# A retention layer feeding a mixer MLP on one core: U ahead of two loads, w1 held and begun narrow, batch 0 in another order

## The chip, the core and the metric

The kernel runs on one core of a Trainium2 chip. A core has five engines with queues of their own, each working through its instructions in the order in which they were written: PE (TensorE, matrix products into PSUM), DVE (VectorE), ACT (ScalarE), POOL (GpSimd) and SP (SyncE, which here only issues DMAs). Semaphores order the engines among each other. The metric is the device time of one execution in microseconds (us); lower is better. The kernel before took 230.05 us (median of 3 runs, 228.76 to 230.13).

## What is computed

Eight heads of 64 columns attend with a decaying state; what comes out is x, 4 batches of 768 positions by 512 columns, and goes through a low-rank mixing over positions and a two-layer MLP with residual:

```python
for t in range(S):                                     # S = 768, H = 8, D = 64
    state = gamma * state + outer(k[:, :, t], v[:, :, t])
    y[:, :, t] = (q[:, :, t] @ state) / sqrt(D)
x  = heads of y side by side                           # 4 x 768 x 512
u  = x + ((x^T @ U) @ V)^T                             # U 768 x 32, V 32 x 768
out = u + relu(u @ w_ch1) @ w_ch2                      # 512 x 2048, 2048 x 512
```

All inputs and the output are float32 in DRAM; the kernel computes in bfloat16 with float32 sums.

## The kernel before

The recurrence is done in chunks: within a chunk by scores between q and k with a mask, across chunks by a state that is carried in PSUM. The decay is put in by scaling k or v by `gk` and q (or x) by `gq`.

Batch 0 is handled apart, since nothing can hide it. It is cut into six units: unit u is a group of four heads (units 0 to 2 and 3 to 5) by 256 positions. `load_unit` puts the loads of k, q and v of each unit, 256 KB each, on SP's queue, in the order of a written string, and U follows as the last. The string `STEPS` then gives all the work of batch 0 in the order in which it is put on the engines, and `BY` says for each step which engine takes it (A is ACT, D is DVE, P is POOL). The steps, with u the unit:

- `Ku`, `Qu`, `Vu` (`cast_unit`): cast the loaded tile to bfloat16; scaled by `gk2` or `gq2` on the way (a two-operand instruction, L83) or plain (L81, L77). The strings `scaled` and `ks` in `BY` say which: q of a unit is scaled where `scaled` has 1, and x is scaled instead where it has 0; k is scaled where `ks` has 1, else v. An S in the V row splits the cast between POOL and DVE (step `Wu`).
- `Tku`, `Tqu`: turn k and q by four matmuls each; `kTu`, `qTu`: bring them out of PSUM.
- `Su`: scores, 16 matmuls into the PSUM pair `R[u % 2]`; `mu`: masks them (DVE, L536).
- `STu.c`, `su.c`: add the half chunk c to the state; bring the state out.
- `Mu`: mix, i.e. state times q and masked scores times v (for unit 5 the part with the state is `N5`, after the rest); `xu`: brings x out.
- `xtc`, `P0`, `P1`, `R2`, `pc0`, `pc2`, `Ec`, `uc`: the low-rank mixing of batch 0, which makes the transposed u that the MLP reads; `Ub` casts U, `Va`, `Vb`, `Vc` bring V into bfloat16 in four copies.
- `Fs:n` (`fill`): n matmuls of zeros by zeros into a tile that step s will write, which keep PE working while it would wait.
- `w0`, `w1`: issue the loads of the columns of `w_ch1` on POOL (`load_w1`, L203). Ahead of the first one a one-element copy, the gate (L691), reads a loaded tile and so holds the load until that tile has landed.
- `B1`, `B2` (`begin_up`, L358): the first matmuls of the MLP of batch 0.

After the steps POOL issues the rest of `w_ch1`, then `w_ch2` in four parts (L208), and then a one-element copy from column 1023 of `w1b` into an input buffer (L712). SP's loads of batch 1 come after it: `feed_more(gate)` writes into that buffer. So batch 1's input starts when POOL has come past its issues and column 1023 has landed. POOL then casts each chunk of 128 positions of batch 1 (`prep`: kd, qd, vd; L81 and L83).

The MLP of a batch is a list of pieces (`mlp_pieces`), each of four matmuls with a cost of 0.864 or 0.432: 16 for the first 512 positions (L380), 16 for the last 256, and 24 of the second layer (L403). `weave` goes through the pieces and puts in, at marks that are fractions of the total cost, the attention of the next batch: `turn_chunk` (L230 for batch 1), `score`, `mix`, and the steps of the mixing. `AT` has for each batch the place of the first score, the step between chunks, and the leads of mix, prep and turn. The store of an output chunk is issued on POOL (L366) one piece after the chunk is complete.

Of the kernel before, what the change touches and what calls it, by code (L numbers as in the profile page):

```python
# [16 lines left out]
def kernel(  # L17
# [11 lines left out]
    nc = tc.nc  # L29
    P = 128  # L30
    B, H, S, D = q.shape
# [26 lines left out]
    R = [psum.tile([P, 2, 512], fp32, tag=f"r{g}", name=f"r{g}") for g in range(2)]  # L58
# [9 lines left out]
    def evac(eng, dst, src):  # L68
        if eng == "A":
            nc.scalar.activation(dst, src, AF.Copy)  # L70
        else:
            nc.vector.tensor_copy(out=dst, in_=src)
# [12 lines left out]
    Ub = wts.tile([P, NCK, RK], bf16)  # L85
    V4 = wts.tile([P, S], bf16)
    w1b = wts.tile([P, NCB, DH], bf16)
# [6 lines left out]
    ready = {}  # L94
    n_in = [0]

    def ring():
        n_in[0] += 1
        return rin.tile([P, 512], fp32, tag="in", name=f"in_{n_in[0]}")

    V1 = wts.tile([RK, S], fp32)
    Uf = wts.tile([P, NCK, RK], fp32)
    nc.sync.dma_start(out=V1, in_=moe_V)

    def load_unit(nm, u):
        g, b0 = UNITS[u]
        t = ready[nm, u] = ring()
        nc.sync.dma_start(
            out=t.rearrange("p (h x) -> p h x", h=HG),
            in_=src_of[nm][0, ds(HG * g, HG), ds(256 * b0, 256), :].rearrange(  # L110
                "h (t j) d -> t h (j d)", j=2))

    for step in ("k0 q0 v0 k1 q1 v1 k2 q2 v2 k3 q3 v3 k4 q4 k5 q5 v4 v5 ").split():
        load_unit(step[0], int(step[1]))
    nc.sync.dma_start(out=Uf, in_=moe_U.rearrange("(j p) r -> p j r", p=P))

    feed = [(nm, b, ci) for b in range(1, B) for ci in range(NCK) for nm in "kqv"]
    n_fed, n_held, n_open = [0], [0], [6 * NCK]
# [14 lines left out]
    def ramp(shape, pattern, mult):  # L133
        n_ramp[0] += 1
        t = consts.tile(shape, fp32, name=f"ramp{n_ramp[0]}")
        nc.gpsimd.iota(t, pattern=pattern, base=0, channel_multiplier=mult,
                       allow_small_or_imprecise_dtypes=True)
        return t
# [20 lines left out]
    s2 = ramp([P, 1], [[0, 1]], 2)  # L159
# [39 lines left out]
        for nm in "kqv":  # L199
            prep(nm, b, ci)  # L200

    def load_w1(mb):
        nc.gpsimd.dma_start(  # L203
            out=w1b[:, :, ts(mb, 512)],
            in_=moe_w_ch1[:, ts(mb, 512)].rearrange("(c p) n -> p c n", p=P))

    def load_w2(j):
        nc.gpsimd.dma_start(  # L208
# [236 lines left out]
    def part(f, *args):  # L445
        return lambda: f(*args)
# [5 lines left out]


    BY = {
             "K": "APADPP",
             "Q": "DDPPPD",
             "scaled": "000010",
             "ks": "010010",
             "V": "PASPDP",
             "kT": "ADAAAA",  # L460
             "qT": "AAAAAA",
             "x": "DDDDAA",
             "s": "AADAAA",
             "pc": "ADA",
             "u": "AAAD",
    }
    STEPS = (
        "Va K0 Q0 Vb Tk0 Vc Tq0 FS0:4 kT0 V0 qT0 S0 K1 ST0.0 FTk1:2 m0 s0.0 "
        "ST0.1 Tk1 s0.1 Q1 M0 V1 kT1 Tq1 ST1.0 FS1:2 qT1 x0 K2 S1 Q2 m1 s1.0 "
        "Tk2 ST1.1 kT2 V2 Tq2 s1.1 W2 M1 qT2 K3 ST2.0 x1 Tk3 S2 FTq3:1 Q3 kT3 "  # L470
        "s2.0 Tq3 FS3:4 m2 V3 qT3 S3 ST3.0 m3 K4 M2 s3.0 ST3.1 s3.1 Q4 Tk4 x2 "
        "M3 FTq4:1 kT4 K5 x3 Tq4 FTk5:1 qT4 Tk5 FTq5:1 Q5 w0 Tq5 kT5 S4 V4 xt0 "
        "w1 qT5 m4 ST4.0 xt1 s4.0 V5 S5 Ub ST4.1 m5 M4 s4.1 ST5.0 x4 P0 M5 s5.0 "
        "pc0 N5 E0 x5 P1 u1 xt2 R2 xt3 u0 pc2 E2 E3 u2 B1 u3 B2 "
    )
    eb = {}
    LAST = NCK - 1
# [1 line left out]
    def cast_unit(nm, u, eng, h0=0, nh=HG):  # L479
        g, b0 = UNITS[u]  # L480
        if (nm, u) not in eb:
            eb[nm, u] = rpre.tile([P, 2, HG, D], bf16, tag=nm + "d",
                                  name=f"{nm}u_{u}")
        src = ready[nm, u].rearrange("p (h j d) -> p j h d", h=HG, j=2)
        scale = gk2 if nm == "kv"[BY["ks"][u] == "0"] else None
        if nm == "q" and BY["scaled"][u] == "1":
            scale = gq2
        hs = ds(h0, nh)
        if scale is not None:
            scale = scale[:, b0, ds(HG * g + h0, nh)].rearrange("p h j -> p j h")  # L490
            scale = scale[:, :, :, None].to_broadcast([P, 2, nh, D])
        cast(eng, eb[nm, u][:, :, hs], src[:, :, hs], scale)
# [24 lines left out]
    def fill(nm, u, n):  # L517
        t = R[u % 2][:, 0] if nm == "S" else turn_bank(nm[1], u)
        for _ in range(n):
            nc.tensor.matmul(t, zeros[:, :P], zeros, start=True, stop=True)  # L520
# [100 lines left out]
    def pc_out(g, eng):  # L621
        rows = ds(2 * RK * g, 2 * RK)
        evac(eng, pcs[0][rows], xT["p"][rows, :P])
# [7 lines left out]
    def step(s):  # L631
        if s[0] == "F":
            s, n = s[1:].split(":")
            return fill(s[:-1], int(s[-1]), int(n))
        if s == "Va":
            return nc.gpsimd.tensor_copy(out=V1b, in_=V1)
        if s == "Vb":
            for i, n in enumerate((512, 256)):
                nc.tensor.matmul(R[1][:, i, :n], rep4, V1b[:, ds(512 * i, n)],
                                 start=True, stop=True)  # L640
            return
        if s == "Vc":
            return evac("D", V4, R[1].rearrange("p i n -> p (i n)")[:, :S])
        nm, at = s.rstrip("0123456789."), s.lstrip("KQVWTkqSmsMNxtPpcERUbuwB")
        u = int(at[0]) if at else 0
        eng = BY[nm][u] if nm in BY and nm != "pc" else None
        if nm in ("K", "Q", "V"):
            if eng == "S":
                cast_unit("v", u, "P", 0, 2)
            else:  # L650
                cast_unit(nm.lower(), u, eng)
        elif nm == "W":
            cast_unit("v", u, "D", 2, 2)
        elif nm in ("Tk", "Tq"):
            turn_unit(nm[1], u)
        elif nm in ("kT", "qT"):
            turned_unit(nm[0], u, eng)
        elif nm == "S":
            score_unit(u)
        elif nm == "m":  # L660
            mask_unit(u)
        elif nm == "ST":
            state_unit(u, int(at[2]))
        elif nm == "s":
            state_out(u, int(at[2]), eng)
        elif nm == "M":
            mix_unit(u)
        elif nm == "N":
            query_unit(u, False)
        elif nm == "x":  # L670
            x_out(u, eng)
        elif nm == "Ub":
            evac("A", Ub, Uf)
        elif nm == "xt":
            x_turn(u)
        elif nm == "P":
            proj(u, range(NCK if u == 0 else 4))
        elif nm == "R":
            proj(1, range(4, NCK))
        elif nm == "pc":  # L680
            pc_out(u // 2, BY["pc"][u // 2])
        elif nm == "E":
            expand((0, 1) if u == 0 else (u,))
        elif nm == "B":
            for m in range(2):
                begin_up(m, (0, 1) if u == 1 else (2,))
        elif nm == "u":
            evac(eng, uTs[0][:, u, :LO], xT[u][:, :LO])
        elif nm == "w":
            if u == 0:  # L690
                nc.gpsimd.tensor_copy(out=gate0, in_=ready["q", 5][:1, :1])  # L691
            load_w1(u)
        else:
            raise ValueError(s)

# [7 lines left out]
    gate0 = consts.tile([1, 1], fp32)  # L703
    pieces0 = mlp_pieces(0)
    for s in STEPS.split():
        step(s)
    for mb in range(2, 4):
        load_w1(mb)
    for j in range(4):
        load_w2(j)  # L710
    gate = ring()
# [4 lines left out]
    for ci in range(3):  # L716
        prep_chunk(1, ci)

    AT = {1: (0.47, 0.068, 0.045, 0.07, 0.04), 2: (0.20, 0.085, 0.05, 0.20, 0.12),
          3: (0.13, 0.10, 0.05, 0.20, 0.12)}  # L720
    LR = (0.71, 0.75, 0.83, 0.89)
    marks = {b: [] for b in range(B)}
# [1 line left out]
    def mark(at, f, *args):  # L724
        marks[int(at)].append((at % 1.0, part(f, *args)))
# [5 lines left out]
    for b in range(1, B):  # L731
        s0, step, dm, dp, dt = AT[b]
        for ci in range(NCK):
            s_at = b - 1 + s0 + step * ci
            if (b, ci) >= (1, 3):
                mark(s_at - dp, prep_chunk, b, ci)
            mark(s_at - dt, turn_chunk, b, ci)
            mark(s_at, score, b, ci)
            mark(s_at + dm, mix, b, ci)
            if b > 2:  # L740
                mark(b - 2 + 0.25 + 0.1 * ci, open_chunk)
        if b == 1:
            mark(0.885, lr_open, b)
            mark(0.885, lr_proj_turn, b)
            mark(0.925, lr_uT, b)
            mark(1.11, lr_expand, b, 0, 4)
        else:
            l0, l1, l2, l3 = LR
            mark(b - 1 + l0, mixed, b)
            mark(b - 1 + l1, lr_expand, b, 0, 4)  # L750
            mark(b - 1 + l2, lr_turn, b, 0)
            mark(b - 1 + l3, lr_turn, b, 2)
        mark(b + 0.02, lr_expand, b, 4, 2)
        mark(b + 0.06, lr_turn, b, 4)
# [35 lines left out]
```

## Time and profile before

One execution was profiled:

| | |
|---|---|
| time of the profiled execution | 229.61 us |
| its span in the profile | 227.8 us |
| median of the 3 timed runs | 230.05 us |
| PE busy in the first 5, second 5, third 5 us | 3.81, 4.76, 4.03 us |
| PE busy, 25 to 30 and 30 to 35 us | 4.87, 5.00 us |
| loads of k, q, v, issue to landing | 4.5, 4.8, 4.6 us (median) |
| loads of w1, issue to landing | 8.2 us (median of 4) |
| loads of w2, issue to landing | 17.6 us (median of 4) |

In the views that follow, a line of the timeline has start and length in us, the engine, the line of the kernel, the operation, the tile written and the tile read with their shapes, how many instructions were merged, and in brackets the idle time of the engine ahead of it with what ended that. Names are those of the tiles: ku, qu, vu are casts of batch 0, kd, qd, vd those of later batches, a the masked scores. The page's rows in tenths cut the span into 40 slices of 5.7 us.

### The profile page before, as it was taken

How to read it: one execution, taken by the hardware profiler on the slowest of the kernel's cores; microseconds unless marked ns; L12 is line 12 of the kernel's file. 1: busy time of each engine (PE TensorE's matmuls, PEld its weight loads, DVE VectorE, ACT ScalarE, POOL GpSimd, SP SyncE). 2: the span in 40 equal slices, each digit the busy share in tenths (PEclk: the TensorE clock that was granted, in tenths of full speed). 3: DMA queues.
4: the chain of work that ended last, by engine and by line, in shares of the span. 5: the costliest groups of instructions: out<-in, count | busy, mean ns of one | idle time of the engine just before them, and what ended most of it. 6: DMA issues, size and time to landing. Idle time of an engine off the chain costs nothing.

```text
span 227.8 us, 4821 instructions
## 1 busy us (share of the span) xinstructions
PE 219.8 (96%) x1984; PEld 122.0 (54%) x1984; DVE 100.2 (44%) x149; ACT 85.2 (37%) x179; POOL 79.4 (35%) x113
## 2 busy tenths in 40 slices
PE   7988999999999999999999999999999999999992
PEld 2556644775555544477544444486544444774451
DVE  5688546255455255454336244443336242222121
ACT  4566554564433235656220035565210044540000
POOL 4569701174691149840100399510101000000110
PEclk9999999999999999999999999999999999999999
DMA  5998999998999998698996644450112530001212
GB/s 174 324 324 132 205 198 198 212 217 201 254 248 261 261 265 178 108 201 180 217 278 176 166 134 95 92 73 1 46 49 73 158 95 0 0 3 46 92 47 92
DMA packets 92374, 34.59 MB, mean 152 GB/s; under 512 B 77360, under 2 KB 90800, under 8 KB 92352
## 3 DMA queue, kind: packets, MB, share of 16 engines
q1 hardware_dynamic: 86224, 23.86, 46.6%
q0 software_dynamic: 6128, 10.42, 18.2%
q8 instruction: 15, 0.25, 0.4%
q14 instruction: 7, 0.06, 0.1%
HBM read 27.46 MB, written 6.29 MB: 148 GB/s over the span
## 4 chain that ended last, share of the span: by engine, by line
PE 50%; issue 34%; POOL 7%; DVE 2%; DMA 2%; ACT 1%; SPq 1%; POOLq 0%; DVEq 0%
PE mlp L380 20%; PE mlp L403 15%; POOL out_dram L366 3%; POOL qd L83 2%; DMA in<-in_q_dram 2%; POOL vd L83 2%; PE mlp L698 2%; PE r L239 1%; PE mlp L503 1%; PE r L260 1%; PE r L529 1%; PE st L271 1%; PE r L255 1%; PE r L584 1%; PE r L302 1%
## 5 line engine op out<-in xcount | busy, mean ns | idle before, releaser
L403 PE MATMUL mlp<-w2b,gT 128*128 128x512 bf16 (+2 forms) x400 | 88.4, 371 | 0.0
L380 PE MATMUL mlp<-uT,w1b 128*128 128x512 bf16 (+1 forms) x506 | 87.4, 325 | 0.3 <-ACT gT L387 0.2
L387 ACT ACTIVATE gT<-mlp 128x512 bf16<-128x512 f32 (+1 forms) x88 | 42.4, 490 | 70.3 <-PE mlp L380 69.2
L380 PEld LDWEIGHTS <-w1b 128*128 128x128 bf16 x506 | 47.8, 98 | 31.9 <-issue 1.0
L403 PEld LDWEIGHTS <-gT 128*128 128x128 bf16 x400 | 36.7, 98 | 38.7 <-issue 0.2
L366 POOL DMA_DIRECT2D out_dram<-o x24 | 13.3, 553 | 112.0 <-DVE o L410 108.6
L385 DVE TENSOR_SCALAR gT<-mlp 128x512 bf16<-128x512 f32 (+1 forms) x40 | 22.2, 556 | 38.0 <-PE mlp L380 38.0
L410 DVE TENSOR_TENSOR o<-mlp,u 128x512 f32<-128x512 f32 (+2 forms) x25 | 16.7, 668 | 37.9 <-PE mlp L403 37.9
L242 DVE TENSOR_TENSOR a<-r,mask 128x1024 bf16<-128x1024 f32 x18 | 22.0, 1223 | 25.6 <-PE r L239 23.1
L83 POOL TENSOR_TENSOR qd<-in,gq 128x512 bf16<-128x512 f32 x18 | 18.7, 1040 | 7.3 <-DMA in<-in_q_dram 7.3
L70 ACT ACTIVATE x<-r 128x512 bf16<-128x512 f32 x19 | 11.3, 597 | 24.3 <-PE r L260 23.3
L83 POOL TENSOR_TENSOR vd<-in,gk 128x512 bf16<-128x512 f32 x18 | 18.7, 1038 | 1.2 <-PE mlp L380 1.1
L81 POOL CAST kd<-in 128x512 bf16<-128x512 f32 x18 | 11.0, 610 | 15.8 <-DMA in<-in_k_dram 10.0
L309 DVE TENSOR_TENSOR u<-r,x 128x512 bf16<-128x512 f32 (+1 forms) x16 | 14.5, 950 | 4.0 <-PE r L302 4.0
L70 ACT ACTIVATE nsz<-st 64x256 bf16<-64x256 f32 x30 | 11.2, 372 | 0.3
L536 DVE TENSOR_TENSOR a<-r,mask 128x1024 bf16<-128x1024 f32 x6 | 7.3, 1224 | 3.2 <-PE r L529 3.1
L239 PEld LDWEIGHTS <-kT 64*128 64x128 bf16 x144 | 4.1, 94 | 6.8 <-issue 5.5
L239 PE MATMUL r<-qT,kT 64*128 64x128 bf16 x144 | 7.2, 219 | 0.0
L260 PE MATMUL r<-vd,a 128*128 128x64 bf16 x144 | 7.1, 193 | 0.0
L260 PEld LDWEIGHTS <-a 128*128 128x128 bf16 x144 | 6.0, 98 | 0.7
L70 ACT ACTIVATE kT<-mlp 128x512 bf16<-128x512 f32 x6 | 3.6, 596 | 7.4 <-PE mlp L230 7.4
L255 PEld LDWEIGHTS <-qT 128*128 128x128 bf16 x60 | 4.6, 98 | 2.5
(106 smaller groups left out, 140.6 us busy)
## 6 DMA issues: line engine op xcount, KB each, us to landing
in<-in_k_dram SPq DMA_DIRECT2D x24, 256.0 KB, 4.5
in<-in_q_dram SPq DMA_DIRECT2D x24, 256.0 KB, 4.8
in<-in_v_dram SPq DMA_DIRECT2D x24, 256.0 KB, 4.6
out_dram<-o POOLq DMA_DIRECT2D x23, 256.0 KB, 2.5
w1b<-in_moe_w_ch_dram POOLq DMA_DIRECT2D x4, 512.0 KB, 8.2
w2b<-in_moe_w_ch_dram POOLq DMA_DIRECT2D x4, 512.0 KB, 17.6
kT<-kd SPq DMA_TRANSPOSE x12, 2.8
qT<-qd SPq DMA_TRANSPOSE x12, 2.4
```

Source lines behind the costliest of these rows:

```text
L70: nc.scalar.activation(dst, src, AF.Copy)
L83: e.tensor_tensor(dst, src, scale, op=ALU.mult)
L239: nc.tensor.matmul(r[:, i, ts(hp, P)], kT[ri, hp], qT[ri, hp], start=True, stop=True)
L242: nc.vector.tensor_tensor(a, r.rearrange("p i (n m) -> p i n m", n=4), mask[:, None, None, :].to_broadcast([P, 2, 4, P]), op=ALU.mult)
L260: nc.tensor.matmul(o[:, ts(h, D)], a[:, i, hp], vb[:, h], start=(ci == 0 and h == 0), stop=True, skip_group_check=True)
L309: nc.vector.tensor_tensor(v4(us[b][:, ds(j0, nj), e]), R[g][:, :, :nj * P].rearrange("p c (j e) -> p c j e", j=nj), v4(xs[b][:, ds(j0, nj) ...
L366: eng.dma_start(out=dst, in_=src)
L380: nc.tensor.matmul(g_p[:, :sz], w1b[:, c, ts(m, P)], uTs[b][:, c, ds(lo, sz)], start=(c == 0), stop=(c == NCB - 1))
L385: nc.vector.tensor_relu(gT[:, m, ds(lo, sz)], g_p[:, :sz])
L387: nc.scalar.activation(gT[:, m, ds(lo, sz)], g_p[:, :sz], AF.Relu)
L403: nc.tensor.matmul(ch[:, :nn], gT[:, m, ts(j, P)], w2b[:, m, ds(n0, nn)], start=(m == 0), stop=(m == NM - 1))
L410: nc.vector.tensor_tensor(o_sb, ch[:, :nn], us[b][:, j, n], op=ALU.add)
```

## The change

U is loaded ahead of the last two loads of v instead of after them. The loads of `w_ch1` are in parts of 256, 256, 512, 512 and 512 columns instead of four of 512, and the gate in front of the first reads v of unit 4 instead of q of unit 5. The engines and the order of batch 0's steps are others: among these DVE has no plain cast of an input any more and scales K0, Q1, K3, K4 and Q5; POOL takes all six V, and V5 stands between the first and the second load of w1; V4 (the tile with four copies of V, step `Vc`) is brought out by ACT instead of DVE; there are 13 fills instead of 16. For batch 1 the first score goes from 0.47 to 0.50 of batch 0's pieces, and three marks of its mixing move by 0.02.

```diff
-    for step in ("k0 q0 v0 k1 q1 v1 k2 q2 v2 k3 q3 v3 k4 q4 k5 q5 v4 v5 ").split():
-        load_unit(step[0], int(step[1]))
-    nc.sync.dma_start(out=Uf, in_=moe_U.rearrange("(j p) r -> p j r", p=P))
+    for step in ("k0 q0 v0 k1 q1 v1 k2 q2 v2 k3 q3 v3 k4 q4 k5 q5 U v4 v5 ").split():
+        if step == "U":
+            nc.sync.dma_start(out=Uf, in_=moe_U.rearrange("(j p) r -> p j r", p=P))
+        else:
+            load_unit(step[0], int(step[1]))
...
-    def load_w1(mb):
+    def load_w1(lo, n):
         nc.gpsimd.dma_start(
-            out=w1b[:, :, ts(mb, 512)],
-            in_=moe_w_ch1[:, ts(mb, 512)].rearrange("(c p) n -> p c n", p=P))
+            out=w1b[:, :, ds(lo, n)],
+            in_=moe_w_ch1[:, ds(lo, n)].rearrange("(c p) n -> p c n", p=P))
...
     BY = {
-             "K": "APADPP",
-             "Q": "DDPPPD",
-             "scaled": "000010",
-             "ks": "010010",
-             "V": "PASPDP",
-             "kT": "ADAAAA",
+             "K": "DPPDDP",
+             "Q": "ADPPPD",
+             "scaled": "011011",
+             "ks": "100111",
+             "V": "PPPPPP",
+             "kT": "DAAAAA",
              "qT": "AAAAAA",
-             "x": "DDDDAA",
-             "s": "AADAAA",
-             "pc": "ADA",
-             "u": "AAAD",
+             "x": "DAADDA",
+             "s": "DAAAAA",
+             "pc": "DAA",
+             "u": "DDDA",
     }
     STEPS = (
-        "Va K0 Q0 Vb Tk0 Vc Tq0 FS0:4 kT0 V0 qT0 S0 K1 ST0.0 FTk1:2 m0 s0.0 "
-        "ST0.1 Tk1 s0.1 Q1 M0 V1 kT1 Tq1 ST1.0 FS1:2 qT1 x0 K2 S1 Q2 m1 s1.0 "
-        "Tk2 ST1.1 kT2 V2 Tq2 s1.1 W2 M1 qT2 K3 ST2.0 x1 Tk3 S2 FTq3:1 Q3 kT3 "
-        "s2.0 Tq3 FS3:4 m2 V3 qT3 S3 ST3.0 m3 K4 M2 s3.0 ST3.1 s3.1 Q4 Tk4 x2 "
-        "M3 FTq4:1 kT4 K5 x3 Tq4 FTk5:1 qT4 Tk5 FTq5:1 Q5 w0 Tq5 kT5 S4 V4 xt0 "
-        "w1 qT5 m4 ST4.0 xt1 s4.0 V5 S5 Ub ST4.1 m5 M4 s4.1 ST5.0 x4 P0 M5 s5.0 "
-        "pc0 N5 E0 x5 P1 u1 xt2 R2 xt3 u0 pc2 E2 E3 u2 B1 u3 B2 "
+        "Va K0 Q0 Vb FTk0:1 Tk0 FTq0:2 Vc V0 Tq0 kT0 ST0.0 FTk1:2 K1 qT0 s0.0 "
+        "ST0.1 Tk1 Q1 S0 kT1 s0.1 Tq1 FTk2:3 V1 m0 qT1 K2 ST1.0 S1 s1.0 Q2 Tk2 "
+        "m1 ST1.1 kT2 M0 V2 s1.1 Tq2 x0 M1 qT2 K3 ST2.0 x1 S2 Q3 m2 Tk3 FTq3:1 "
+        "s2.0 kT3 V3 Tq3 qT3 ST3.0 M2 K4 s3.0 S3 x2 ST3.1 m3 Q4 Tk4 FTq4:3 s3.1 "
+        "kT4 K5 Tq4 M3 FTk5:1 qT4 Q5 Tk5 Ub S4 kT5 x3 Tq5 V4 xt0 qT5 m4 w0 "
+        "ST4.0 xt1 s4.0 S5 ST4.1 V5 m5 M4 s4.1 w1 ST5.0 P0 s5.0 x4 M5 pc0 N5 E0 "
+        "x5 P1 u0 xt2 R2 xt3 u1 pc2 E2 E3 u2 B1 u3 B2 "
     )
...
         if s == "Vc":
-            return evac("D", V4, R[1].rearrange("p i n -> p (i n)")[:, :S])
+            return evac("A", V4, R[1].rearrange("p i n -> p (i n)")[:, :S])
...
             if u == 0:
-                nc.gpsimd.tensor_copy(out=gate0, in_=ready["q", 5][:1, :1])
-            load_w1(u)
+                nc.gpsimd.tensor_copy(out=gate0, in_=ready["v", 4][:1, :1])
+            load_w1(256 * u, 256)
...
-    for mb in range(2, 4):
-        load_w1(mb)
+    for mb in range(1, 4):
+        load_w1(512 * mb, 512)
...
-    AT = {1: (0.47, 0.068, 0.045, 0.07, 0.04), 2: (0.20, 0.085, 0.05, 0.20, 0.12),
+    AT = {1: (0.50, 0.068, 0.045, 0.07, 0.04), 2: (0.20, 0.085, 0.05, 0.20, 0.12),
           3: (0.13, 0.10, 0.05, 0.20, 0.12)}
...
-            mark(0.885, lr_open, b)
-            mark(0.885, lr_proj_turn, b)
-            mark(0.925, lr_uT, b)
+            mark(0.905, lr_open, b)
+            mark(0.905, lr_proj_turn, b)
+            mark(0.945, lr_uT, b)
```

## The prediction

> **What bounds it now.** I read the page first (busy times and slices), then the chain of waits in order of time, then the timeline of the first 30 us, then POOL, PE and the DMA queues between 26 and 70 us.
>
> ```profile
> PE 219.8 (96%) x1984; PEld 122.0 (54%) x1984; DVE 100.2 (44%) x149; ACT 85.2 (37%) x179; POOL 79.4 (35%) x113
> PE   7988999999999999999999999999999999999992
> PEclk9999999999999999999999999999999999999999
> ```
>
> PE is full from the fifth slice to the last, at the full granted clock. Of its 8 idle us, about 4 lie behind the last matmul; from 27 to 223 us stand only some 0.25 us near 64, 0.25 near 142 and crumbs. So the end is the start of the MLP of batch 0 (step B1) plus a fixed amount of PE work plus stalls. The change can move the start and the stalls, not the work.
>
> ```profile
> 13.36 1.07 POOL L83 TENSOR_TENSOR vu<-in,gk 128x512 bf16<-128x512 f32 x1 [0.20 <-DMA in<-in_v_dram]
> 13.44 1.27 DVE L81 CAST ku<-in 128x512 bf16<-128x512 f32 x1
> ...
> 17.95 1.70 POOL L203 DMA_DIRECT2D w1b<-in_moe_w_ch_dram  x2
> ...
> 19.91 1.12 DVE L81 CAST qu<-in 128x512 bf16<-128x512 f32 x1
> ...
> 21.88 2.47 DVE L536 TENSOR_TENSOR a<-r,mask 128x1024 bf16<-128x1024 f32 x2 [0.52 <-PE r L529]
> ...
> 27.21 1.47 PE L358 MATMUL mlp<-uT,w1b 128*128 128x512 bf16 x6
> ```
>
> This is the timeline (start, length). The late half hangs on Q5: its DVE cast ends at 21.03, though its data landed at 17.6 (issue 11.93 plus 5.7 to landing), so the masks of units 4 and 5 run back to back until 24.35, and B1 starts 2.86 us later, at 27.21.
>
> ```profile
> 26.22 0.17 POOL L712 CAST in<-w1b 1x1 f32<-1x1 bf16 x1 [0.84 <-DMA w1b<-in_moe_w_ch_dram]
> 37.80 0.61 POOL L81 CAST kd<-in 128x512 bf16<-128x512 f32 x1 [10.02 <-DMA in<-in_k_dram]
> 44.84 1.04 POOL L83 TENSOR_TENSOR qd<-in,gq 128x512 bf16<-128x512 f32 x1 [6.43 <-DMA in<-in_q_dram]
> ```
> ```profile
> 46.62 0.39 PE L230 MATMUL mlp<-ident,kd 128*128 128x128 bf16 x4
> ```
>
> POOL's and PE's timelines: batch 1's input is let go at 26.22 and crawls beside the weights; its first q is cast at 45.88, and PE turns it at 46.85. That slack of 1 us is all there is.
>
> **The start, walked.** Each step begins when its engine, in the new written order, and its data are ready, 0.05 us after the releaser (mask 21.88 after a score that ended at 21.83). Lengths from rows: POOL cast 0.61, POOL scaling 1.05; ACT turned k 0.60, turned q 0.75, state 0.38, x 0.60; DVE mask 1.22, 512-column op 0.69; PE turn 0.33, score 0.35, state half 0.24, mix 0.34 plus 0.33 for a query pair, fill 0.22. Two have no row. DVE's 512-column scaling of an SBUF input: 256 columns took 0.42, and x from PSUM 0.68; I take 0.69. V4's evacuation on ACT (768 columns): between 0.60 for 512 and 1.02 for 1024, so 0.82; it ends near 6.85 and is read first at E0, so it only delays turned q 0, to 7.5.
>
> The inputs land as before up to q5. The new order gives scores S0 to S3 at 9.1, 10.7, 13.4 and 16.1 (before 7.8, 11.5, 15.1, 16.9): later at first, because K0 is scaled and three fills stand ahead, then earlier. From there q4's landing leads, where POOL began its scaling at 16.29:
> - POOL: Q4 to 17.35, K5 to 18.4, V4 (landing 18.4 before, plus 0.4 for U, the gap between the landings of v5 and U) 18.85 to 19.46, gate copy 0.18, first w1 issue 19.65 to 20.5, V5 to 21.1.
> - PE: Tq4 17.75, M3 18.1, a fill, Tk5 18.78 to 19.1. ACT: turned q 4 until 18.9, Ub 0.36 (U's landing has moved up from 19.5, since it now precedes v4), so S4 19.1, turned k 5 to 19.86, Tq5 19.8, turned q 5 to 20.61.
> - DVE: Q5 to 19.09, x3 to 19.77, m4 to 20.99. S5 20.7 to 21.05, m5 21.1 to 22.32.
> - Tail: x4 23.0, pc0 23.29, E0 23.34; N5 ends 23.31, x5 on ACT 23.96, R2 24.57, pc2 24.89, E2 and E3 to 25.27, B1 25.27. From m5's end that is 2.95 us; before it was 2.86.
>
> So B1 moves up by 27.21 - 25.27 = 1.94 us. The three fills fewer (13 for 16) are in the walk. The walk has no spare for jitter: 0.5 worse is possible, and 0.35 better if K3 below meets no block.
>
> The contention row is the cast pair quoted above: DVE's cast took 1.27 beside POOL's op and ended 0.28 after it, against 0.41 for the cast of V5 at 20.94. After, DVE does no such cast, but scales K0, Q1, K3, K4 and Q5. The one scaling on DVE before (256 columns, 13.11) met POOL for 0.05 us and then 0.17 and shows no block. I take the dearer end, a wait for POOL's running op: K3 goes from 13.05 to 13.5, Q5 from 17.75 to 18.4, and both are in the times above. The cheaper end saves the 0.35. The Trainium skill, "SBUF — State Buffer", section "Who interferes with whom", speaks against the new placing: it says that a DVE instruction with two SBUF inputs and a GpSimd instruction that reads SBUF exclude each other for a whole instruction. By it the dearer end holds at both places; no run here shows it for a scaling.
>
> **w1.** The gate's wait for v4 adds nothing: V4's cast stands ahead of it on POOL and waits for the same load. On SP U's issue (0.66) passes two loads that land by the order of transfers, the 0.4 above. Before, issue at 17.95 gave first bytes at 19.7 (the DMA queues by window: 0.21 MB until 21.5, then 1.63 MB in 8 us, 0.205 MB/us). After, issue 19.65 gives 21.4; 0.25 MB, with the 0.4 lost in the ramp and 0.65 to the landing, is there at 23.8, before B1. The second 256 columns (issue 21.1, behind V5, which itself waits behind the first issue) land at 25.1, m2 needs them at 27.3; columns 512 to 1023 at 27.6, needed at 29.0. Cost nothing; if a 0.5 KB packet takes as long as one of 1 KB (97 ns: the weights' queue held 123.4% of 16 engines for those 8 us, over 1636 packets) they come 2.5 us later, a stall of about 1.2 at m4.
>
> **What is late next: batch 1's input.** Behind V5 POOL issues 1 + 3 loads of w1 at 0.87 and four of w2 (2.99 in all): 27.6. The copy on L712, which lets the input go, follows at 27.7, 1.5 later than 26.22. Until the weights are through, the input gets 0.51 MB in 13 us (window 30.5 to 43.5: 0.039 MB/us; the weights 0.155). Weights begin 1.7 later, so the slow stretch ends later as well; q of chunk 0 lands 1.5 later, at 46.3, and is scaled at 47.4.
>
> PE's turn of it: batch 0's pieces sum to 16 x 0.864 + 16 x 0.432 + 24 x 0.864 = 41.47. The mark moves from (0.47 - 0.04) x 41.47 = 17.83, taken at 18.14, to 19.08, taken at 19.44: 1.30 later in work. PE is there at 46.62 - 1.94 + 1.30 = 45.98, turns k, and stands from 46.2 to 47.45: 1.25 lost. Later turns: chunk 1 at 51.6 against 51.2, chunk 2 at 55.7 against 54.7, chunk 3 at 59.9 against 59.0. The stall of 0.24 at 64.27 (POOL's prep for chunk 4 stands behind the store of the second output) leaves chunk 4, whose turn now comes 0.86 later behind that store, but the same geometry comes up for chunk 5 behind the third: even.
>
> Sum: -1.94 + 1.25 = -0.7 on the profiled execution's 229.61, or 228.9; that execution lies 0.44 under the median of 230.05, so 229.3. Other marks (0.885 to 0.905, 0.925 to 0.945) move with the mixing they follow and leave two pieces, 1.73, for the evacuations of up to 1.2 us: nothing.
>
> **Rivals.**
> - *The input comes no later* (the queues share otherwise than I reckon). For it: the first 256 columns keep the weights short; against: the gate copy is plainly later. Then only the 1.94 count: 228.1; with the cheaper contention end 227.75.
> - *The narrow loads are slow and the input starves; slower than before.* Place: the turn of chunk 0 of batch 1. Price: 2.5 us later landing, stall 3.75, net +1.8, so 231.9. It turns into a loss when q lands after 47.0 (a stall of 1.94; 2.2 us later than now). For it: the copy that lets the input go now stands behind V5 and nine issues, where eight stood; against: the 0.5 KB packets of the first input took 26 ns (103.6% of 16 engines over 16 us, 10204 packets), so a packet costs by its size.
> - *The start is not shortened* (blocks on DVE, the order itself): B1 near 27, PE at 47.7, no stall: 230.0.
>
> **Numbers.** Forecast 0.50 (229.3, own range 228.4 to 230.2), input not late 0.20, starvation 0.18, no shorter start 0.12. The range 227.9 to 231.9 leaves out about 2 in 10: the better end of the first rival and the worse half of the second. A change under 1% (2.3 us) I call the same: faster needs 227.75, the first rival's far end and a little of the forecast, 0.15; slower needs 232.35, starvation worse than priced and a start later than before, 0.14; same 0.71.
>
> **What would show it.** B1 at 25.3 (over 26.5: the walk is wrong; look at the DVE scalings beside POOL); m5 ending at 22.3; the L712 copy (now L714) near 27.7; POOL's first qd at 46.3; PE idle some 1.2 us there. A stall at the second group of w1 columns, or a granted clock under full, would make the sum wrong.

## The result and the profile after

The changed kernel took 231.78 us (median of 6 runs, 230.48 to 232.96) against 229.97 for the kernel before on the same chip. The ratio is 1.0097 with a 95% interval of 1.0071 to 1.0123: slower by about 1%. The profiled execution took 231.68 with a span of 229.9 us, 2.1 more than before. Executions more than 1.5% above the fastest of their kernel are left out of the ratios: three of nine for e17 (six took 227.2 to 228.7 us, the three 232.3 to 232.5), three of ten for e16, two for e5 and one each for e4, e6, e14 and e18; the profiled ones of e6, e17 and e18 are among them.

The page of the changed kernel, busy tenths of PE and granted clock:

```profile
PE   7899999959999999999999999999999999999992
PEclk9999999979999999999999999999999999999999
```

PE has a hole in the ninth slice (46 to 52 us), and the clock sinks in the same slice. Neither was there before. The timeline shows that the start itself went as it was walked:

```profile
12.70 0.68 DVE L83 TENSOR_TENSOR ku<-in,gk 128x512 bf16<-128x512 f32 x1
12.86 1.00 POOL L81 CAST qu<-in 128x512 bf16<-128x512 f32 x1
...
17.54 1.05 POOL L83 TENSOR_TENSOR ku<-in,gk 128x512 bf16<-128x512 f32 x1
17.86 1.28 DVE L83 TENSOR_TENSOR qu<-in,gq 128x512 bf16<-128x512 f32 x1 [0.52 <-DMA in<-in_q_dram]
...
19.82 0.93 POOL L205 DMA_DIRECT2D w1b<-in_moe_w_ch_dram  x1
20.75 0.62 POOL L81 CAST vu<-in 128x512 bf16<-128x512 f32 x1
...
21.08 1.22 DVE L538 TENSOR_TENSOR a<-r,mask 128x1024 bf16<-128x1024 f32 x1 [0.21 <-PE r L531]
25.11 1.47 PE L360 MATMUL mlp<-uT,w1b 128*128 128x512 bf16 x5
```

The mask of unit 5 ends at 22.30 and B1 starts at 25.11, 2.10 us ahead of the profiled execution before. What follows is late. POOL's and PE's timelines:

```profile
28.75 0.18 POOL L714 CAST in<-w1b 1x1 f32<-1x1 bf16 x1 [1.50 <-DMA w1b<-in_moe_w_ch_dram]
41.38 0.61 POOL L81 CAST kd<-in 128x512 bf16<-128x512 f32 x1 [11.07 <-DMA in<-in_k_dram]
47.98 1.04 POOL L83 TENSOR_TENSOR qd<-in,gq 128x512 bf16<-128x512 f32 x1 [6.00 <-DMA in<-in_q_dram]
```
```profile
45.83 0.39 PE L232 MATMUL mlp<-ident,kd 128*128 128x128 bf16 x4
49.08 0.61 PE L232 MATMUL mlp<-ident,qd 128*128 128x128 bf16 x4 [2.86 <-POOL qd L83]
```

PE turns k of chunk 0 of batch 1 at 45.83, 0.8 us earlier than before, and then waits 2.86 us for q, which landed 3.1 us later than before. The stages around it (length, then busy time of PE, PEld, DVE, ACT and POOL, granted clock, DMA):

```profile
44.94:48.35 3.41, 1.27 (x14) 1.00 (x12) 0.42 (x1) 1.42 (x4) 0.37 (x1) 1.00 1.23 224
48.35:51.77 3.42, 2.69 (x15) 2.02 (x16) 1.11 (x2) 0.35 (x1) 2.48 (x4) 0.50 0.84 190
```

When PE resumes, the granted clock is 0.50 until 51.77: 2.69 us of work at half speed, some 1.35 us lost by estimate. The account of this execution: -2.10 at B1, +2.86 stall, +1.35 clock, and +0.26 as a wait of 0.5 near 63 us (second layer behind ACT's turned k) takes the place of the 0.24 near 64. That is +2.4 where the spans differ by 2.1.

The clock's term is not in every execution. The mean granted clock was 1.00 in three of the six (230.48, 231.46 and 232.15 us) and 0.991 to 0.993 in the other three (231.68, 231.88 and 232.96). The first three took 0.8 us less in the mean, and yet 1.5 more than the mean of the kernel before: most of the loss is there at full clock.

### The profile page after: what moved, and what is told of

The parts are those of the page before. It is cut to its first block, busy times and chain, and to the rows that moved or that the text cites. A ratio compares the mean times of both kernels' runs of the same rounds, so it can differ in the third digit from the quotient of the medians.

```text
span 229.9 us, 4791 instructions
## 1 busy us (share of the span) xinstructions
PE 217.5 (95%) x1956; PEld 122.6 (53%) x1981; DVE 99.5 (43%) x148; ACT 84.8 (37%) x177; POOL 80.7 (35%) x116
## 3 DMA queue, kind: packets, MB, share of 16 engines
q0 software_dynamic: 6656, 10.42, 18.6%
## 4 chain that ended last, share of the span: by engine, by line
PE 44%; issue 32%; DMA 13%; POOL 7%; SPq 1%; DVE 1%; POOLq 0%; ACT 0%; ACTq 0%
PE mlp L405 18%; PE mlp L382 14%; DMA in<-in_q_dram 8%; DMA w1b<-in_moe_w_ch_dram 3%; POOL out_dram L368 3%; DMA in<-in_v_dram 2%; PE r L241 2%; POOL qd L83 1%; PE r L262 1%; PE mlp L232 1%; PE st L273 1%; PE r L257 1%; POOL vd L83 1%; PE mlp L505 1%; POOL vu L81 1%
## 5 line engine op out<-in xcount | busy, mean ns | idle before, releaser
L382 PE MATMUL mlp<-uT,w1b 128*128 128x256 bf16 (+1 forms) x500 | 87.9, 328 | 0.6 <-ACT gT L389 0.2
L405 PE MATMUL mlp<-w2b,gT 128*128 128x512 bf16 (+2 forms) x384 | 86.9, 370 | 1.5 <-ACT kT L70 0.5
L382 PEld LDWEIGHTS <-w1b 128*128 128x128 bf16 x506 | 48.5, 99 | 32.1 <-issue 0.8
L70 ACT ACTIVATE x<-r 128x512 bf16<-128x512 f32 x21 | 12.5, 597 | 24.2 <-PE r L262 22.5
L72 DVE CAST qT<-mlp 128x512 bf16<-128x512 f32 x6 | 4.1, 687 | 4.4 <-PE mlp L232 4.3
## 6 DMA issues: line engine op xcount, KB each, us to landing
w2b<-in_moe_w_ch_dram POOLq DMA_DIRECT2D x4, 512.0 KB, 18.5
```

Of the source, the lines that this page charges most:

```text
L382: nc.tensor.matmul(g_p[:, :sz], w1b[:, c, ts(m, P)], uTs[b][:, c, ds(lo, sz)], start=(c == 0), stop=(c == NCB - 1))
L405: nc.tensor.matmul(ch[:, :nn], gT[:, m, ts(j, P)], w2b[:, m, ds(n0, nn)], start=(m == 0), stop=(m == NM - 1))
```

## The experiments

Ratios are to the kernel before, run beside each kernel. The times in the table are from one profiled execution of each kernel. The first w1 byte is where packets of that queue begin to flow (in e9, e16 and e18 a few come up to 0.5 us earlier), "copy" is the one-element copy that lets batch 1's input go, "q" the start of POOL's scaling of the first q, "turn" PE's turn of the first k, "stall" PE's waits for batch 1's prepared k and q (POOL) at its turns.

| kernel | first w1 byte | copy | q | turn | stall | ratio, interval |
|---|---|---|---|---|---|---|
| before | 19.7 | 26.2 | 44.8 | 46.6 | 0.2 | 1 |
| changed | 21.5 | 28.8 | 48.0 | 45.8 | 2.9 | 1.0097, 1.0071 to 1.0123 |
| e1 | 21.0 | 28.6 | 47.5 | 45.5 | 2.7 | 1.0025, 0.9999 to 1.0050 |
| e2 | 21.4 | 28.7 | 47.7 | 45.7 | filled | 1.0056, 1.0026 to 1.0086 |
| e3 | 21.1 | 28.5 | 47.5 | 44.4 | 4.1 | 1.0193, 1.0142 to 1.0244 |
| e4 | 20.0 | 28.4 | 47.3 | 46.0 | 2.3 | 1.0058, 1.0013 to 1.0104 |
| e5 | 20.7 | 30.1 | 47.7 | 47.0 | 1.3 | 1.0069, 1.0030 to 1.0107 |
| e6 | 21.9 | 24.7 | 44.2 | 47.5 | 0.6 | 1.0024, 0.9984 to 1.0064 |
| e7 | 20.5 | 24.5 | 44.0 | 45.0 | 1.7 | 0.9985, 0.9957 to 1.0012 |
| e8 | 22.3 | 26.2 | 45.0 | 47.0 | 1.1 | 1.0047, 1.0017 to 1.0077 |
| e9 | 22.0 | 28.9 | 47.6 | 45.5 | 3.1 | 1.0068, 1.0028 to 1.0108 |
| e10 | 20.8 | 29.2 | 47.2 | 45.1 | 3.1 | 1.0091, 1.0052 to 1.0130 |
| e11 | 20.1 | 28.5 | 47.0 | 45.8 | 1.9 | 1.0008, 0.9976 to 1.0039 |
| e12 | 18.5 | 25.6 | 44.6 | 46.1 | 0.2 | 0.9976, 0.9954 to 0.9999 |
| e13 | 21.7 | 29.4 | 48.3 | 46.3 | 2.7 | 1.0091, 1.0053 to 1.0128 |
| e14 | 20.9 | 28.9 | 47.5 | 45.8 | 2.3 | 1.0078, 1.0036 to 1.0120 |
| e15 | 21.1 | 28.4 | 47.8 | 45.9 | 2.6 | 1.0064, 1.0026 to 1.0103 |
| e16 | 18.2 | 26.2 | 44.2 | 49.2 | 0 | 1.0021, 0.9978 to 1.0064 |
| e17 | 15.8 | 27.5 | 45.9 | 50.5 | 0 | 0.9941, 0.9913 to 0.9969 |
| e18 | 17.9 | 29.5 | 47.7 | 50.6 | 0.2 | 1.0101, 1.0058 to 1.0144 |

**e1, wide parts.** In the changed kernel:

```diff
-            load_w1(256 * u, 256)
+            load_w1(512 * u, 512)
-    for mb in range(1, 4):
+    for mb in range(2, 4):
```

> The changed kernel with w1 in four parts of 512 columns again, all else kept. Theory N (the two narrow loads hold the DMA engines longer per byte: 70 ns a packet of 0.5 KB against 97 ns for 1 KB): the copy that lets batch 1's input go comes near 27.3 instead of 28.75 us, the first q of batch 1 lands near 46.5 instead of 48.0, PE stands about 1.4 us at its turn instead of 2.86, the granted clock stays at 1.0 behind it, and the time falls by 2.5 to 3 us, to about 229. Rival H (only the hold until v of unit 4 counts, the width nothing): first q at 48.0, time within 0.5 us of the changed kernel's 231.8.

229.99 us: the ratio falls from 1.0097 to 1.0025, and the intervals are apart, so the narrow parts cost the changed kernel some 0.7%. The profiled execution doesn't show how. It is one of the two slowest of the ten (231.56 and 231.58, the other eight 229.5 to 230.2), with the copy only 0.2 us earlier than in the changed kernel, q at 47.5 rather than 46.5, and the half clock behind the stall. The mean granted clock was 0.993 in these two and 0.999 to 1.00 in the eight, and one window of 3.41 us at half clock, some 1.7 us of work, is about their distance. When q landed in the eight no trace shows.

**e2, the stall filled with work.** In `turn_chunk`:

```diff
+            for _ in range(12 if (nm, b, ci) == ("q", 1, 0) else 0):
+                nc.tensor.matmul(tp, zeros[:, :P], zeros, start=True, stop=True)
```

> The changed kernel with 12 matmuls of zeros (2.6 us at full clock) between the turns of k and q of batch 1's chunk 0, where PE stands idle. Theory C (the idle itself costs 2.86 us and the half clock behind it 1.36 more): the stall stays, the clock stays at 1.0, and the time falls by 1.2 to 1.5 us, to about 230.4. Rival: the drop of the clock is not the idle's doing or costs nothing: no change, 231.8.

The input came as late as in the changed kernel, the clock stayed at 1.00 until 226.8 us, and the ratio fell to 1.0056, 0.41% or 0.9 us less than the changed kernel's, under the 1.2 to 1.5 expected. As only half of the changed kernel's executions had the lower clock, less was to be had. The intervals overlap (1.0071 to 1.0086), so the gain itself is not clear of noise.

**e3, the marks at 0.47.** `AT` and the three marks of batch 1 are as in the kernel before.

> The changed kernel with batch 1's marks as before (0.47, 0.885, 0.925). Theory: q of chunk 0 lands when the DMA queues have it, so PE comes to the turn 1.3 us earlier, waits until the same 49.1 us, and has 1.3 us more work left: about 233.1. Rival (the later marks are themselves what costs, by pushing batch 1's attention into the second layer): 231.8 or less.

```profile
44.36 0.39 PE L232 MATMUL mlp<-ident,kd 128*128 128x128 bf16 x4
48.56 0.61 PE L232 MATMUL mlp<-ident,qd 128*128 128x128 bf16 x4 [3.82 <-POOL qd L83]
```

The timeline of e3 has PE there 1.5 us earlier, and q scaled only 0.5 us earlier (47.5). It took 233.97 us, 0.9 more than expected: in the profiled execution the clock was down behind the hole for two windows of 3.41 us instead of one. PE's earliness is worth nothing here; the later marks are what the change does right.

**e4, the narrow parts alone, in the kernel before.** 

> The kernel before with w1 in parts of 256, 256, 512, 512, 512 at the same places, nothing else changed. Theory N: the letting go of batch 1's input comes 1 to 1.5 us later than 26.2, the first q lands near 46, which uses up the 1 us of slack there: 0.2 to 0.6 us slower than 230.0. Rival H: no change in either.

230.38 us, 1.0058. In the profiled execution the first byte came at 20.0, about as before, but the copy, whose column is now in the third load, at 28.4 instead of 26.2, and q at 47.3 instead of 44.8. The delay is more than expected, in the way expected, and the ratio says that the width costs something by itself. But this execution (232.51) is one of four at 231.9 to 233.9, and the other six took 229.7 to 230.6; how late q was in those is not shown.

**e5, the hold undone.** The hold is the gate's wait for v of unit 4. Here the gate reads q of unit 5 again, and `w0` stands ahead of `V4`.

> The changed kernel with the gate of the first w1 load on q of unit 5 again and its issue ahead of the cast of V4; order, widths and marks kept. Theory F (batch 1's input is let go too late, and each part of the change that delays it adds): the first issue comes near 18.7 instead of 19.8 us, the first q of batch 1 near 47.0 instead of 48.0, PE stands 1.9 us instead of 2.9, and the half clock behind it mostly goes: 229.3 to 230.8. Rival W (the weights and v then collide and the units get later): B1 after 25.5, time not below 231.5.

The ratio is 1.0069, with executions from 229.5 to 233.4. The issue came 0.8 us earlier, the copy later (30.1), and PE waited 0.5 us on w1 as well. The interval overlaps the changed kernel's: the hold alone is not shown to cost anything.

**e6 to e8, the input let go earlier.** The copy stands ahead of the four w2 issues and reads a column of the first w1 load, in the changed kernel (e6), in the kernel before (e7), and in e1's (e8).

```diff
-    for j in range(4):
-        load_w2(j)
     gate = ring()
-    nc.gpsimd.tensor_copy(out=gate[:1, :1], in_=w1b[:1, NCB - 1, 1023:1024])
+    nc.gpsimd.tensor_copy(out=gate[:1, :1], in_=w1b[:1, NCB - 1, 255:256])
     feed_more(gate)
+    for j in range(4):
+        load_w2(j)
```

> The changed kernel with the copy that lets batch 1's input go put ahead of the four w2 issues and reading column 255 (first w1 load) instead of 1023. Theory F: the copy comes near 24.4 instead of 28.75 us, the first q lands near 42, the stall at its turn and the half clock are gone, PE runs on from B1 at 25.1: about 227.5, faster than the kernel before. Rival B (the DMA engines are the bound, so w1 and w2 now come late by as much): stalls of 2 us or more at w1 or w2 instead, 230 or more.

> The kernel before with the same copy ahead of the w2 issues, reading column 511. Theory F: its q lands early enough as it is (1 us of slack), so an earlier input gives nothing: within 0.5 us of before. Rival B: 1 us or more slower, as weights come late. A gain over 0.7 us would mean that the kernel before is held there as well.

> As the changed kernel with the earlier copy, and w1 in four parts of 512 columns (copy reads column 511). Theory F: once the input is early the width has nothing left to delay: within 0.4 us of the one with the narrow loads, near 227.5. Rival N2 (the narrow first load starts the MLP earlier or later by itself): a difference over 0.5 us, seen at B1.

POOL's timeline of e6:

```profile
24.69 0.18 POOL L712 CAST in<-w1b 1x1 f32<-1x1 bf16 x1
44.23 1.04 POOL L83 TENSOR_TENSOR qd<-in,gq 128x512 bf16<-128x512 f32 x1 [5.93 <-DMA in<-in_q_dram]
```

q of chunk 0 was scaled at 44 to 45 us in all three, and they took 230.72, 229.41 and 230.75. e6's interval lies wholly below the changed kernel's: letting the input go earlier, with nothing else changed, takes back some 0.7%. That is the plainest sign that the late input is what costs. It is far from the 227.5 that was expected, though. e6's profiled execution (232.99, the highest of ten) waits 1.2 us on w1 and 0.6 at the turn of chunk 1, e8's 0.5 on w1 and 1.1 at that turn: as rival B has it, what is served earlier delays the rest. e7 fits rival B less well. It waits 1.7 at chunk 1, but its B1 was at 25.62, and it is level with the kernel before, not 1 us or more slower. This led to theory D, that a later first byte of the weights is a later end.

**e9, a later first byte in the kernel before.** The gate reads v of unit 5. 

> The kernel before with the gate in front of its first w1 issue reading v of unit 5 (landing near 19.1 us) instead of q of unit 5 (17.6). Theory D (from the first byte of w1 until batch 1's first chunks have landed the DMA engines are the bound, some 25.5 us from first byte to v of chunk 0, so a later first byte is a later end): first byte 1.2 to 1.5 us later, stalls of PE at the turns of chunk 0 or 1, 0.7 to 1.5 us slower than before. Rival P (the slack takes it up): within 0.3 us of before.

```profile
45.48 0.39 PE L230 MATMUL mlp<-ident,kd 128*128 128x128 bf16 x4
48.73 0.40 PE L230 MATMUL mlp<-ident,qd 128*128 128x128 bf16 x4 [2.87 <-POOL qd L83]
```

This is e9's timeline. One edit of the gate, 2.3 us on the first byte, reproduces the changed kernel's stall in the old order: 231.30 us, 1.0068. The profiled execution (232.89) is the second slowest of the ten, which run from 229.97 to 233.15, so its stall need not be the usual size.

**e10, e11, the new order with the loads of before.** U is last, w1 is in four parts, and the gate reads q of unit 5; on POOL, V4 stands between the first two w1 issues, where the kernel before has nothing. The marks are at 0.47 (e10) and at 0.50 (e11).

> Batch 0's new order with the loads of before: U last (its cast moved behind the state 4.0 for that), w1 in four parts of 512, gate on q of unit 5, first issue ahead of V4, second behind V4, marks at 0.47. Theory D: B1 near 25.2, but the DMA queue ends as in before, so PE waits at the turns for what it gained: 229.2 to 230.2, no faster than before. Rival P (PE's earlier start is what counts once the loads are as before): 228.6 or less.

> The same with batch 1's marks at 0.50 as in the change. Theory D: PE comes to the turn of chunk 0 1.3 us later in its work, when the data are nearly there; 0.5 to 1.3 us less than with 0.47, 228.4 to 229.2. Rival: the marks make no difference, as the same data are waited for at chunk 1.

The ratios are 1.0091 and 1.0008. B1 came at 25.7 and 25.0, and no gain is left: q was scaled at 47.2 and 47.0. e10 is even slower than the kernel before, 1.6 us over the expected level; its copy came at 29.2 though its first byte was at 20.8. Why the copy is so late is not shown. It came 6.5 us behind the first byte in the kernel before and 6.9 in e9, but 7.1 to 9.4 in the changed kernel, e1 to e5 and e10 to e16, and neither the width nor a cast between the first two issues sorts these: e15, wide and with the issues one behind the other, took 7.3, e14, narrow, 8.0, and e1, wide with a cast between, 7.6.

**e12, an earlier first byte in the kernel before.** The gate reads k of unit 4, `w0` stands ahead of `Q4`. 

> The kernel before with the gate on k of unit 4 and the first w1 issue ahead of Q4 on POOL, some 2 us earlier. Theory D: the weights fill the gap between the last input and the first w1 byte (0.9 us before) and the stretch ends earlier by 0.5 to 1 us; with B1 late by up to 1 us as v comes later, the time is within 0.7 us of before, on the lower side. Rival P: only the later inputs count, 0.5 us or more slower.

```profile
16.77 0.93 POOL L203 DMA_DIRECT2D w1b<-in_moe_w_ch_dram  x1
...
25.56 0.18 POOL L712 CAST in<-w1b 1x1 f32<-1x1 bf16 x1
```

In e12, whose POOL timeline this is, the first byte came at 18.5, there was no stall but 0.2, and the time was 229.06 us against 229.59, a ratio of 0.9976 (0.9954 to 0.9999). That is on the side that theory D expects, but the trace does not put it down to the theory: q was scaled only 0.2 us earlier than before (44.6), the stall is the same, and B1 was 0.5 earlier (26.71). So of the two tests e9 speaks for theory D and e12 leaves it open. The table speaks for a narrower reading. q follows the copy by 17.6 to 19.5 us in all twenty kernels, and the first byte by anything from 22.3 (e6) to 30.1 (e17): in these traces q goes by when the input is let go, and the first byte counts as far as it moves that.

**e13 to e15, what inside the change delays.** U is last (e13), or the second w1 issue stands right behind the first, with narrow parts (e14) and wide ones (e15).

> The changed kernel with U loaded last again (and its cast moved behind the state 4.0, so that ACT does not wait for it). If U ahead of v delays the last inputs: last input byte 0.5 to 1 us earlier than the changed kernel's 20.05, first w1 byte and first q of batch 1 earlier by as much, and 0.5 to 1.5 us less than 231.8. If it is harmless: within 0.4 us of 231.8.

> The changed kernel with the second w1 issue right behind the first, ahead of the cast of V5; widths kept. Theory G (the 256-column load is through before the second is there, and the DMA queue runs dry for most of 1 us): no dip in the bytes of the weights' queue, first q of batch 1 0.6 to 1 us earlier, 0.5 to 1.5 us less than 231.8; V5 0.9 us later moves B1 by up to 0.7. Rival (packets of 0.5 KB are what costs): within 0.4 us of 231.8.

> The same with four parts of 512 columns. Theory G: little more to gain, within 0.5 us of the narrow one. Rival (0.5 KB packets): 0.5 to 1 us less than the narrow one, as 0.5 MB at 68 ns a packet instead of 99 ns for twice the bytes is 0.75 us of 16 engines.

All three intervals overlap the changed kernel's. No cost of U ahead is seen (1.0091; the last byte of v came 0.8 us earlier, the first w1 byte did not). For e14 and e15 nothing can be told: their difference of 0.14% is well inside either interval. The gap between the two narrow loads is in the trace, in the DMA rates (GB/s) of the changed kernel from 21.4 to 25.4, in slices of 0.1 us, with the share of the engines above:

```profile
DMA  2999999999999999962590296799999999999999
GB/s 31 97 113 108 174 179 200 195 189 215 184 225 184 189 174 139 205 26 5 36 31 10 36 77 82 102 128 159 148 184 143 174 184 184 205 195 200 164 149 128
```

The first load, 0.25 MB, is through at 23.1, and the second, issued behind V5, brings its first full rate near 24: some 0.8 us with few bytes moved. That it costs time is not shown, as e14 has no clear gain.

**e16 to e18, the new order with an early first byte.** e16 is as e12 with the new order and U last, e17 has U ahead as in the change, and e18 is e17 with the marks at 0.47. In all three w1 is in four parts. The edit of e17, without that of the parts:

```diff
-        "... m3 Q4 Tk4 FTq4:3 ... x3 Tq5 V4 xt0 qT5 m4 w0 ... s4.1 w1 ST5.0 ..."
+        "... m3 w0 Q4 Tk4 FTq4:3 ... x3 Tq5 w1 V4 xt0 qT5 m4 ... s4.1 ST5.0 ..."
-                nc.gpsimd.tensor_copy(out=gate0, in_=ready["v", 4][:1, :1])
+                nc.gpsimd.tensor_copy(out=gate0, in_=ready["k", 4][:1, :1])
```

> The new order and marks with U last, w1 in parts of 512, and its first issue ahead of Q4 with the gate on k of unit 4 (as in e12), the second ahead of V4. Theory D: first byte near 18.5, first q of batch 1 near 45, B1 at 25.5 to 26, PE at the turn 46.2 to 46.7: no stall, 228.3 to 229.0, level with e12 or below it. Rival: POOL's Q4 and K5, 0.9 us later, take the order's gain: 229.5 or more.

> The changed kernel with w1 in four parts of 512, the first issue ahead of Q4 with the gate on k of unit 4, the second ahead of V4; U, order and marks as in the change. Theory D: first w1 byte near 17.5, first q of batch 1 near 44.5, B1 near 25.3, no stall at the turn of chunk 0 and full clock: 227.3 to 228.5, faster than the kernel before. Rival (the order gives nothing even then): 229.0 or more.

> The same with batch 1's marks at 0.47. If its input is just in time at 0.50, PE comes 1.3 us too early here and waits: 0.3 to 1.3 us more than e17, perhaps with the half clock behind it. If the input is early enough: within 0.3 us of e17.

e16 (230.92, executions from 227.7 to 235.5) doesn't test what it was made for. U starved beside w1, and ACT, which casts it in its order, held PE, as its timeline has it:

```profile
23.15 0.36 ACT L70 ACTIVATE Ub<-Uf 128x192 bf16<-128x192 f32 x1 [2.59 <-DMA Uf<-in_moe_U_dram]
...
23.84 0.31 PE L552 MATMUL st<-vu,ku 64*64 64x64 bf16 x8 [2.24 <-ACT s L70]
```

With U ahead, e17 gives 0.9941 (0.9913 to 0.9969), the best of the kernels here, but for six executions of nine. In its profiled one, which is not among the six, the early w1 collided with the last inputs (last input byte at 22.0 instead of 20.05), B1 came at 29.3 and the clock was at half from 23.6 to 30.4. Over all nine the mean is 229.45 us against 229.32 for the kernel before, so the gain is not safe, and no trace shows how the six came by it. e18 at 1.0101 can't be put down to the earlier marks: its profiled execution has the same collision and a stall at the turn of only 0.2, and the mean granted clock was 0.981 to 0.989 in five of its six executions, as in e17's slower three (0.981 to 0.990).

## Why the prediction was wrong

The sign was wrong: 229.3 was forecast, 231.78 measured, near the 231.9 of the second rival, which had a chance of 0.18.

- *The start* held: POOL's issue 19.82 for 19.65, m5's end 22.30 for 22.32, B1 25.11 for 25.27. The dearer end for the contention held too. DVE's scaling of Q5 took 1.28 us instead of 0.68 beside POOL's K5 and ended 0.55 behind it, and at K3 it was POOL's cast that took 1.00 instead of 0.61. The Trainium skill, "SBUF — State Buffer", "Who interferes with whom", has this exclusion, and the trace agrees, both ways round. The row that I cited as the cast of V5 at 20.94 was that of V4; the length was right.
- *The gain was read off one execution.* In the other kernels with the old order B1 came at 25.6 (e7), 26.1 (e9), 26.6 (e4) and 26.7 (e12); 27.21 was the late end. The new order is worth less than 1.94, 0.5 to 1.6 us against these.
- *The step that failed is "What is late next: batch 1's input".* It was the right place, priced too low three times. The copy came at 28.75 for 27.7, because it waited not for POOL's issues (through at 27.3) but 1.5 us longer for column 1023; I had written that the narrow parts "cost nothing" and that "a packet costs by its size". A packet of 0.5 KB took 68 ns in the mean and one of 1 KB about 100, so by estimate half a megabyte in narrow parts takes 16 engines some 1.2 us longer (1024 packets x 68 ns / 16 = 4.35 us against 512 x 100 / 16 = 3.20), and the queue ran nearly dry for 0.8. How much of the copy's lateness these two make is open, since it came at 28.6 in e1's trace, where the parts are wide and the rate, once up, does not fall under 126 GB/s. q landed near 48.0 for 46.3, 19.2 us behind the copy where before it was 18.6, and the stall was 2.86 for 1.25. And the half clock behind it, 1.35 us in the profiled execution and by the granted clock there in half of them, was in no term.
- *The rival of starvation* had the mechanism, the place and nearly the price (+1.8); it lacked the clock and had a landing 0.8 us too late. These two offset each other, so that 231.9 came so near is in part luck. I gave it too little because the copy's wait was reckoned from the mean rate of the queue and not from the landing of one load.
- *The slack* was seen (1 us) and the DMA stretch was seen; what I did not draw from them is that between first w1 byte and about 48 us PE's start hardly counts. e9 shows that holding the weights back is enough to bring the stall, e6 that letting the input go earlier takes most of the loss away, and e10 and e11 that the new order with the loads of before gains nothing.

What stays open is how the 1% splits among hold, gap and width. Of the single edits of the changed kernel only the widths' reversal (e1) and the earlier copy (e6) stand clear of it on the better side, while e15, wide as well, does not.

## What to carry to other kernels

When a prologue is shortened, ask what the engine will meet next, and when that was set in motion: here a DMA-bound stretch that begins with the weights, and in it the moment at which the next input is let go. Holding a transfer back so that a neighbour lands sooner can move what is queued behind it (e9). An engine that arrives earlier at data that are late gains nothing, and with the marks at 0.47 it lost 0.8 to 1% (e3 against the changed kernel, e10 against e11). Price a stall of a few us on PE with what the clock may do after it.

## What the runs showed of the hardware

The granted clock can fall for a window of 3.41 us or two after a window in which PE stood still for part of it (1.2 to 2.9 us in these traces); whether one stall does it depends in part on where it lies. These windows lie in whole steps of 3.41 us from the steps of each run's own clock; they are of e4, e11, e14, e16 and e17, in this order, with the same columns as above:

```profile
45.84:49.25 3.41, 1.40 (x18) 1.15 (x16) 0.41 (x1) 1.19 (x3) 1.89 (x2) 1.00 1.01 221
49.25:52.66 3.41, 3.41 (x23) 2.14 (x22) 1.45 (x4) 0.77 (x2) 2.87 (x5) 0.50 1.12 253
```
```profile
44.70:48.12 3.42, 1.50 (x17) 1.22 (x15) 0.42 (x1) 1.59 (x4) 1.05 (x2) 1.00 0.96 204
48.12:51.50 3.38, 3.33 (x30) 2.16 (x32) 1.45 (x3) 0.77 (x2) 3.02 (x4) 1.00 1.02 231
```
```profile
44.64:48.06 3.42, 1.58 (x17) 1.28 (x14) 0.43 (x1) 1.67 (x5) 0.61 (x1) 1.00 1.19 229
48.06:51.47 3.41, 2.87 (x28) 1.96 (x30) 1.02 (x2) 0.77 (x2) 3.21 (x5) 1.00 1.06 240
```
```profile
22.63:26.04 3.41, 2.20 (x54) 1.57 (x54) 0.75 (x3) 1.62 (x4) 1.75 (x3) 1.00 1.25 209
26.04:29.45 3.41, 3.19 (x18) 1.30 (x17) 1.56 (x3) 0.87 (x2) 1.56 (x4) 0.50 1.24 203
```
```profile
23.56:26.98 3.42, 3.42 (x63) 2.35 (x64) 1.78 (x4) 1.18 (x3) 3.42 (x6) 0.50 0.89 128
26.98:30.39 3.41, 3.41 (x25) 1.53 (x22) 1.91 (x3) 0.87 (x2) 2.08 (x5) 0.50 1.23 201
```

With PE busy for 1.40 us of the window the clock halved (e4, and 1.27 in the changed kernel); with 1.50 and 1.58 it did not. e15's stall of 2.6 us, split over two windows (1.99 and 2.18 us busy), left it at full, while e4's of 2.0 did not. But PE's busy time does not decide alone: in e16 the clock halved after a window with 2.20 us busy. Nor does it for the way back up. A window with 2.69 us busy was enough in the changed kernel and 2.10 was not in e3, but in e17 a window with PE busy throughout was followed by another at half clock. The windows of e16 and e17 hold many small matmuls of the end of batch 0; whether that is why is not shown.

The Trainium skill, "TensorE: Matmul & The Clock Gate", Part 1, puts the drop after at least one idle window. The traces here differ: no window ahead of a drop was idle, PE was busy in them for 0.54 us (e9) to 2.20 (e16).

The two DMA queues that share the engines sent packets about one for one while both had work. From 32 to 45 us of the changed kernel the weights sent 2015 packets and the input 1877, but 2.00 against 0.48 MB, as the input's packets have 256 bytes; from 30.5 to 43.5 us of the kernel before it was 2020 and 2018 packets, 2.01 and 0.51 MB. So the input crawls beside the weights, and q took until 48 us.
